# Final adds one output tile later on VectorE, and the last transposes between the two filler pairs

## The chip, the cores and the metric

The kernel runs on one core of one Trainium2 chip. Times are device microseconds (us) of that core. TensorE does matmuls, VectorE, ScalarE and GpSimd do elementwise work, SyncE issues most of the transfers.

Two measures are used. The first is the median device time of several runs. The second is the **tail**, read from the timeline of one profiled execution: it begins at the start of the "first late reciprocal" (the first RECIPROCAL over 2 columns, line L693), which runs when the last attention block is done, and it is read to the end of the last VectorE add and on to the end of the span. The page prints the span to 0.1 us, but the view of a window that runs to the end of the span gives that end to 0.01 us, and the tables and the text use that.

## The reference, cut to what matters

```python
xn = _layernorm(x, axis=-1)                       # x: 1 x 2048 x 512
s  = attention(xn, k_cache, v_cache, wq, wo)      # 32 heads of 128, 2048 keys, then @ wo
g  = silu(relu_glu_mlp(xn, W_gate, W_up, W_down))
return x + s * g
```

The 2048 rows are 16 output tiles of 128 x 512. The heads are worked in 8 groups of 4. For seven groups the projection with `wo` is accumulated in SBUF and folded into `x_sb` early (`x + s_acc * g`). For the last group each output tile is finished by itself: four matmuls into PSUM, a multiply by `g`, an add onto `x_sb`, a store.

## The kernel before

Tiles 0 to 7 of this final stage are mixed into the last attention blocks. Tiles 8 to 15 come after them. Tiles 12 to 15 need the output of the very last attention block, which must be normalised on VectorE, transposed on TensorE and copied to SBUF on ScalarE; tiles 8 to 11 do not need it and serve as filler for TensorE meanwhile.

```python
fin_tmp = [S_([128, D], BF16, "fin_tmp") for _ in range(2)]
# ... (cut)
def emit_final_tile(n, bank):
    # ... (waits, cut)
    for hh in range(G):
        ins = pe.matmul(ps_r[:, bank, 0:D], OT_store[gL % 2][:, hh, n*128:(n+1)*128],
                        Wo_sb[gL % 2][:, hh, :], start=(hh == 0), stop=(hh == G - 1))
    otok = sem_op.sig(ins)
    fb = fin_cnt[0] % NFT                         # NFT = len(fin_tmp)
    fin_cnt[0] += 1
    _wait(dve, otok)
    _wait(dve, fin_free[fb])
    mtok = sem_opa.sig(
        dve.tensor_tensor(fin_tmp[fb][:], ps_r[:, bank, 0:D], g_sb[:, n, :], ALU.mult))   # L787
    _wait(dve, mtok)                              # the add waits for the multiply in front of it
    ftok = sem_opa.sig(
        dve.tensor_tensor(x_sb[:, n, :], x_sb[:, n, :], fin_tmp[fb][:], ALU.add))         # L792
    fin_free[fb] = ftok
    # ... then the store of the tile, or of a pair of tiles, from SyncE
    return mtok                                   # frees the PSUM bank

# ... (cut) after the last attention block:
for n in range(NT - 8, NT - 4, 2):                # tiles 8 to 11, the fillers
    emit_M([(emit_final_tile, n), (emit_final_tile, n + 1)])
flush_last_transposes()                           # TensorE transposes, ScalarE copies
for n in range(NT - 4, NT, 2):                    # tiles 12 to 15
    emit_M([(emit_final_tile, n), (emit_final_tile, n + 1)])
```

`emit_M` takes one of three PSUM slots of two banks each, and waits until its last readers are done.

The softmax here doesn't subtract the row's maximum and nothing guards it: scores larger than these inputs give would overflow.

## Time and profile before

| what | value | view |
|---|---|---|
| median of the first three runs | 1287.48 us (1286.75 to 1287.56) | run times |
| span of the profiled run | 1286.0 us | page |
| share of the chain that ended last on TensorE | 98% | page, part 4 |
| VectorE busy over the whole span | 382.0 us, 30% | page, part 1 |
| VectorE in the tail | from 1274.27 to 1283.91 without a gap | timeline |
| TensorE's last matmul of the tail ends | 1282.08 | timeline |
| end of the span | 1285.96 | window to the end of the span |

The shares over the whole span say "TensorE". They are an average over stages. The final tiles run in the last 30 us (tile 0's multiply starts at 1255.91), what the change can save lies in the last 12, and only the timeline of those tells what limits them. This is VectorE's timeline before the change; columns: start in us, length in us, engine, line and operation, output and inputs, count, and in brackets idle time before it and what ended it. Onorm is the normalised output of the last attention block.

```profile
1274.27 0.17 DVE L693 RECIPROCAL rz_sb<-ps_acc 128x2 f32<-128x2 f32 x1 [0.35 <-PE ps_acc L742]
1274.48 0.42 DVE L696 TENSOR_TENSOR Onorm<-ps_acc,rz_sb 128x256 bf16<-128x256 f32 x1
1274.82 0.16 DVE L693 RECIPROCAL rz_sb<-ps_acc 128x2 f32<-128x2 f32 x1
1275.01 0.42 DVE L696 TENSOR_TENSOR Onorm<-ps_acc,rz_sb 128x256 bf16<-128x256 f32 x1
1275.35 0.68 DVE L787 TENSOR_TENSOR fin_tmp<-ps_r,g_sb 128x512 bf16<-128x512 f32 x1
1276.07 0.42 DVE L792 TENSOR_TENSOR x_sb<-x_sb,fin_tmp 128x512 bf16<-128x512 bf16 x1
1276.41 0.68 DVE L787 TENSOR_TENSOR fin_tmp<-ps_r,g_sb 128x512 bf16<-128x512 f32 x1
...
1282.78 0.68 DVE L787 TENSOR_TENSOR fin_tmp<-ps_r,g_sb 128x512 bf16<-128x512 f32 x1
1283.49 0.42 DVE L792 TENSOR_TENSOR x_sb<-x_sb,fin_tmp 128x512 bf16<-128x512 bf16 x1
```

Read the starts, not only the lengths. From a multiply to its own add it is 1276.07 - 1275.35 = 0.72 us, more than the multiply's 0.68: the add waits for the result. From that add to the next multiply it is 1276.41 - 1276.07 = 0.34 us, less than the add's recorded 0.42: the next operation waits for nothing and starts before the record of this one ends. One tile takes 1.06 us. What 0.72 could be is shown elsewhere in the same trace, where VectorE works through independent operations of the same length back to back, 0.59 to 0.60 us from start to start (the Trainium skill, "Perfetto Trace Analysis", section "DVE / Act Engine Instruction", says that the record runs until the write is acknowledged, while the next operation may begin its fetch earlier). VectorE's timeline before the change, in the first stage:

```profile
21.72 0.67 DVE L460 TENSOR_TENSOR hT<-gr_sb,ps_r 128x512 bf16<-128x512 bf16 x1
22.31 0.69 DVE L319 BATCH_NORM_STATS2 stats<-x_sb 128x6 f32<-128x512 bf16 x1
22.91 0.67 DVE L460 TENSOR_TENSOR hT<-gr_sb,ps_r 128x512 bf16<-128x512 bf16 x1
```

TensorE's timeline before the change, over the same tail:

```profile
1274.19 3.62 PE L779 MATMUL ps_r<-Wo_sb,OT_store 128*128 128x512 bf16 x16
1277.64 0.39 PE L714 MATMUL ps_r<-ident,Onorm 128*128 128x128 bf16 x4
1278.47 3.61 PE L779 MATMUL ps_r<-Wo_sb,OT_store 128*128 128x512 bf16 x16 [0.44 <-ACT OT_store L719]
```

Tiles 8 to 11 (16 matmuls), the four transposes, a wait of 0.44 us for ScalarE's copies, tiles 12 to 15. TensorE is done at 1282.08, while VectorE begins the multiply of the last tile only at 1282.78. TensorE's wait is therefore not what ends the kernel, before the change.

### The profile page before, as it was taken

How to read it: one execution, taken by the hardware profiler on the slowest of the kernel's cores; microseconds unless marked ns; L12 is line 12 of the kernel's file. 1: busy time of each engine (PE TensorE's matmuls, PEld its weight loads, DVE VectorE, ACT ScalarE, POOL GpSimd, SP SyncE). 2: the span in 40 equal slices, each digit the busy share in tenths (PEclk: the TensorE clock that was granted, in tenths of full speed). 3: DMA queues.
4: the chain of work that ended last, by engine and by line, in shares of the span. 5: the costliest groups of instructions: out<-in, count | busy, mean ns of one | idle time of the engine just before them, and what ended most of it. 6: DMA issues, size and time to landing. Idle time of an engine off the chain costs nothing.

```text
span 1286.0 us, 26948 instructions
## 1 busy us (share of the span) xinstructions
PE 1279.3 (99%) x12040; PEld 835.4 (65%) x12040; DVE 382.0 (30%) x685; ACT 1001.7 (78%) x1109; POOL 13.2 (1%) x25
## 2 busy tenths in 40 slices
PE   9999999999999999999999999999999999999998
PEld 5444466666666666666666666666666666666665
DVE  6433311112222222222222222222222222234456
ACT  3322399998888888888888888888888888888884
POOL 2100000000000000000000000000000000000000
PEclk9999999999999999999999999999999999999999
DMA  9600123332222332332221322323323212332302
GB/s 262 131 1 1 21 44 52 63 57 38 37 54 47 71 54 50 55 70 51 54 46 33 64 47 53 55 67 55 55 50 71 54 34 38 52 65 55 50 14 74
DMA packets 240977, 72.13 MB, mean 56 GB/s; under 512 B 227808, under 2 KB 240864, under 8 KB 240864
## 3 DMA queue, kind: packets, MB, share of 16 engines
q1 hardware_dynamic: 240048, 69.76, 28.4%
q8 instruction: 96, 1.57, 0.5%
q10 hardware_dynamic: 816, 0.66, 0.2%
q14 instruction: 17, 0.14, 0.0%
HBM read 32.77 MB, written 2.10 MB: 27 GB/s over the span
## 4 chain that ended last, share of the span: by engine, by line
PE 98%; DVE 1%; DMA 0%; issue 0%; ACT 0%; ACTq 0%
PE ps_acc L742 36%; PE ps_r L645 34%; PE ps_r L578 9%; PE ps_r L599 8%; PE ps_acc L511 4%; PE ps_r L488 4%; PE ps_r L492 4%; PE ps_r L779 1%; DMA Wu_sb<-in_B_W_up_dram 0%; DVE fin_tmp L787 0%; PE ps_r L402 0%; ACT gr_sb L454 0%; DVE x_sb L792 0%; PE ps_acc L364 0%; DVE Onorm L696 0%
## 5 line engine op out<-in xcount | busy, mean ns | idle before, releaser
L655 ACT ACTIVATE PT<-ps_r 128x1024 bf16<-128x1024 f32 x1024 | 952.5, 1054 | 167.7 <-PE ps_r L645 167.7
L742 PEld LDWEIGHTS ps_acc<-V_sb,PT 128*128 128x128 bf16 x8192 | 621.1, 98 | 241.7 <-ACT PT L655 3.5
L742 PE MATMUL ps_acc<-V_sb,PT 128*128 128x129 bf16 x8192 | 776.7, 220 | 0.0
L645 PE MATMUL ps_r<-QT_sb,KT_sb 128*128 128x512 bf16 x2048 | 754.2, 379 | 0.0
L672 DVE RECIPROCAL rz_sb<-ps_acc 128x4 f32<-128x4 f32 x127 | 23.3, 184 | 729.5 <-PE ps_acc L742 729.5
L645 PEld LDWEIGHTS ps_r<-QT_sb,KT_sb 128*128 128x128 bf16 x2048 | 194.9, 98 | 1.1 <-DVE QT_sb L589 0.4
L578 PE MATMUL ps_r<-xnT,Wq_sb 128*128 128x512 bf16 x512 | 130.9, 379 | 0.0
L599 PE MATMUL ps_r<-Wo_sb,OT_store 128*128 128x512 bf16 x448 | 114.6, 379 | 0.0
L589 DVE CAST QT_sb<-ps_r 128x512 bf16<-128x512 f32 x128 | 88.5, 692 | 48.1 <-PE ps_r L578 48.1
L578 PEld LDWEIGHTS ps_r<-xnT,Wq_sb 128*128 128x128 bf16 x512 | 49.9, 97 | 60.6 <-ACT PT L655 27.1
L675 DVE TENSOR_TENSOR Onorm<-ps_acc,rz_sb 128x512 bf16<-128x512 f32 x127 | 87.8, 691 | 4.4
L599 PEld LDWEIGHTS ps_r<-Wo_sb,OT_store 128*128 128x128 bf16 x448 | 43.8, 98 | 52.9 <-ACT PT L655 0.2
L454 ACT ACTIVATE gr_sb<-ps_r 128x512 bf16<-128x512 f32 x56 | 32.9, 595 | 49.9 <-PE ps_r L488 49.3
L612 DVE TENSOR_TENSOR s_acc<-s_acc,ps_r 128x512 f32<-128x512 f32 x96 | 66.0, 688 | 17.3 <-PE ps_r L599 17.3
L460 DVE TENSOR_TENSOR hT<-gr_sb,ps_r 128x512 bf16<-128x512 bf16 x56 | 38.4, 686 | 47.2 <-PE ps_r L492 42.1
L511 PE MATMUL ps_acc<-Wd_sb,hT 128*128 128x512 bf16 x224 | 49.0, 379 | 0.0
L492 PE MATMUL ps_r<-xnT,Wu_sb 128*128 128x512 bf16 x168 | 43.1, 379 | 0.0
L488 PE MATMUL ps_r<-xnT,Wg_sb 128*128 128x512 bf16 x168 | 43.1, 379 | 0.0
L511 PEld LDWEIGHTS ps_acc<-Wd_sb,hT 128*128 128x128 bf16 x224 | 21.9, 98 | 26.4
L519 ACT ACTIVATE sig_sb<-ps_acc 128x512 f32<-128x512 f32 x12 | 7.2, 597 | 29.5 <-PE ps_acc L511 29.5
L488 PEld LDWEIGHTS ps_r<-xnT,Wg_sb 128*128 128x128 bf16 x168 | 16.4, 98 | 19.8
L492 PEld LDWEIGHTS ps_r<-xnT,Wu_sb 128*128 128x128 bf16 x168 | 16.4, 98 | 19.8
(50 smaller groups left out, 182.2 us busy)
## 6 DMA issues: line engine op xcount, KB each, us to landing
V_sb<-in_A_v_cache_dram SPq DMA_DIRECT2D x32, 512.0 KB, 4.8
Wq_sb<-in_A_wq_dram SPq DMA_DIRECT2D x32, 128.0 KB, 2.5
Wo_sb<-in_A_wo_dram SPq DMA_DIRECT2D x8, 512.0 KB, 5.0
OT_store<-Onorm SPq DMA_TRANSPOSE x127, 2.4
Wd_sb<-in_B_W_down_dram SPq DMA_DIRECT2D x1, 1792.0 KB, 14.3
x_sb<-in_A_x_dram SPq DMA_DIRECT2D x3, 512.0 KB, 11.4
out_dram<-x_sb SPq DMA_DIRECT2D x6, 256.0 KB, 2.2
Wg_sb<-in_B_W_gate_dram SPq DMA_DIRECT2D x1, 768.0 KB, 10.9
```

The lines of the kernel that those rows point to most:

```text
L460: dve.tensor_tensor(hT[par][:, fc, :], gr_sb[gk][:], ps_r[:, gb + 1, :], ALU.mult)
L488: ins = pe.matmul(ps_r[:, gb, :], Wg_sb[:, c, fs], xT[:, c, xs], start=(c == 0), stop=(c == DC - 1))
L492: ins = pe.matmul(ps_r[:, gb + 1, :], Wu_sb[:, c, fs], xT[:, c, xs], start=(c == 0), stop=(c == DC - 1))
L511: ins = pe.matmul(ps_acc[:, jb, 0:D], hT[par][:, fc, j * 128:(j + 1) * 128], Wd_sb[:, fc, :], start=(fc == 0), stop=(fc == FC - 1))
L578: ins = pe.matmul(ps_r[:, bank, :], Wq_sb[b][:, c, :], xnT[:, c, qs], start=(c == 0), stop=(c == DC - 1))
L589: etok = sem_qpe.sig(dve.tensor_copy(QT_sb[b][:, qs], ps_r[:, bank, :]))
L599: ins = pe.matmul(ps_r[:, bank, 0:D], OT_store[g % 2][:, hh, n * 128:(n + 1) * 128], Wo_sb[g % 2][:, hh, :], start=(hh == 0), stop=(hh == ...
L612: dve.tensor_tensor(s_acc[:, n, :], s_acc[:, n, :], ps_r[:, bank, 0:D], ALU.add)
L645: ins = pe.matmul(ps_r[:, 2 * s + tt, :], KT_sb[h % 2][:, t * 128:(t + 1) * 128], QT_sb[h % 2][:, qs], start=True, stop=True)
L655: act.activation(PT[pb][:], ps_r[:, 2 * s:2 * s + 2, :], ACTF.Exp, scale=scale)
L675: dve.tensor_tensor(Onorm[ob][:], o_ap, rz_sb[:].to_broadcast([128, 4, Dh]), ALU.mult))
L742: ins = pe.matmul(o_ap, PT[pb][:, tt, j * 128:(j + 1) * 128], V_sb[vb][:, t, 0:VW], start=(t == 0 and j % 2 == 0), stop=(t == KT - 1 and j ...
```

## The change

Its intent: no add shall wait for the operation right in front of it, and TensorE shall not wait for the copies. The number of operations stays the same.

```diff
-fin_tmp = [S_([128, D], BF16, "fin_tmp") for _ in range(2)]
+fin_tmp = [S_([128, D], BF16, "fin_tmp") for _ in range(4)]
@@ in emit_final_tile, after the multiply of tile n
+                    flush_final_add()                 # the add of the tile before
+                    fin_pending.append((n, fb, mtok))
+                    return mtok
+
+                fin_pending = []
+
+                def flush_final_add():
+                    if not fin_pending:
+                        return
+                    n, fb, mtok = fin_pending.pop()
+                    Q, j = divmod(n, 4)
                     _wait(dve, mtok)
                     # ... add and store as before, cut
-                    return mtok
@@ the end of the kernel
                 for n in range(NT - 8, NT - 4, 2):
                     emit_M([(emit_final_tile, n), (emit_final_tile, n + 1)])
-                flush_last_transposes()
+                    if n == NT - 8:
+                        flush_last_transposes()
                 for n in range(NT - 4, NT, 2):
                     emit_M([(emit_final_tile, n), (emit_final_tile, n + 1)])
+                flush_final_add()
```

## The prediction

> **What bounds the kernel now.** The chain of waits puts 98% of the 1286.0 us span on TensorE; the change touches only the last 30 us. There VectorE bounds the end. By the timeline it runs without a gap from 1274.27 to 1283.91 us: reciprocal, Onorm, reciprocal, Onorm, then eight pairs (tiles 8 to 15) of multiply L787 (0.68 us) and add L792 (0.42 us), one tile every 1.06 us. TensorE's last output matmul ends at about 1282.08; the last store lands about 2.1 us after the last add.
>
> **Where the time is in a pair.** Start to start, multiply to its own add takes 0.72 us. Add to the next, independent multiply takes 0.345 us although the add is recorded at 0.42: independent neighbours overlap by about 0.08. Elsewhere in this trace (batch-norm statistics and hT products, 20 to 30 us) an independent successor of a 0.69 us operation starts 0.60 us after it, a dependent one 0.72. The Trainium skill, "VectorE: DVE Perf Modes", section "The DRAIN you can't avoid", says that a semaphore between chained operations costs nothing extra; this trace disagrees by 0.11 us per dependent pair.
>
> **What the change does.** No operation is added or removed. (1) Each add comes one multiply later, so no add but the last waits for the operation right before it. The cadence should fall from 1.06 to 0.60 + 0.345 = 0.95 us per tile; TensorE needs 4 x 0.216 = 0.86, so VectorE stays the limit, barely. (2) The add of tile 7, which now runs before an idle gap of 0.35 us, is pushed behind the multiply of tile 8, into the saturated stretch: plus 0.35. (3) The last transposes (0.23 us on TensorE) go eight matmuls earlier, so the ScalarE copies (0.65 us) hide behind tiles 10 and 11; TensorE loses its wait of 0.44 to 0.6 us near 1278 and ends at about 1281.5. That wait is off the critical path today, but after (1) a late TensorE would become the limit: (3) is what lets (1) pay.
>
> **Sum**, an estimate from these numbers: multiply of tile 8 at 1275.35 as before; then one every 0.95 us, the last at 1282.0; add 14 at 1282.6; add 15 at 1282.95, ending at about 1283.37 instead of 1283.91: 0.54 us less. (Eight tiles x 0.11 = 0.88, less 0.35 for the displaced add.) Adds 14 and 15 are then 0.35 us apart instead of 1.06; one store issue takes SyncE 0.33 us and 128 KB take about 0.5 us at the 253 GB/s seen in the window, so the last store may wait for the one before: give back 0.1 to 0.2 us. Net 0.4 us, to 1287.1 us: 0.03%, less than the spread of the three runs before (0.8 us). Tiles 0 to 7 run in VectorE's slack and give nothing.
>
> Range 1286.3 to 1287.8. Faster by over 2%: 1%; within 2%: 98%; slower by over 2%: 1%.
>
> **What would show it.** Right: multiplies 0.95 us apart in the tail's timeline, adds starting 0.60 after the unrelated multiply, TensorE continuous from 1274.2 to about 1281.5 with the copies under tiles 10 and 11, the last add ending 9.1 us after the first late reciprocal starts, where it was 9.64. Wrong: multiply to add still 0.72 (the change then loses 0.35 us); VectorE idle behind output matmuls; transposes held up by the second Onorm (it ends at 1275.43, TensorE gets there near 1275.9).
>
> **What would make it wrong.** An overlap that holds for other pairs but not for multiply to add; a last store that queues for longer; drift of the whole program by more than the gain.

## The result

| | before | after |
|---|---|---|
| median | 1287.5 us (1286.75 to 1287.57, 6 runs) | 1286.69 us (1286.24 to 1287.28, 6 runs) |
| span of the profiled run | 1285.96 | 1284.64 |
| start of the first score matmul | 144.85 | 144.06 |
| from there to the first late reciprocal | 1129.42 | 1129.42 |
| tail to the last add | 9.64 | 8.96 |
| tail to the end of the span | 11.68 | 11.16 |

The ratio of the times is 0.9995, with a 95% interval from 0.9982 to 1.0008. It is the mean of one kernel's fast runs over that of the other's of the same rounds, so not quite the ratio of the medians. By this alone the kernels are the same. The tail is clearer: it is 0.68 us shorter to the last add and 0.52 us shorter to the end. The two profiled spans differ by more, 1.32 us; the table shows that 0.79 us of that was there before the first score matmul, in code that the change does not touch. Most of it, 0.66 us, comes from one wait; 0.12 us is there one group of matmuls earlier (6.33 against 6.21). TensorE's timeline before the change, at the start of the kernel:

```profile
7.23 0.40 PE L402 MATMUL ps_r<-xcT,Wu_sb 128*128 128x128 bf16 x4 [0.51 <-DMA Wu_sb<-in_B_W_up_dram]
```

and after the change:

```profile
6.45 0.39 PE L402 MATMUL ps_r<-xcT,Wu_sb 128*128 128x128 bf16 x4
```

The first up-weights had landed earlier in that run (5.1 us after their issue, 6.0 before the change). From there on the two executions keep a constant distance of 0.79 us until the tail begins (144.85 against 144.06, 1274.27 against 1273.48).

VectorE's timeline after the change:

```profile
1273.48 0.17 DVE L693 RECIPROCAL rz_sb<-ps_acc 128x2 f32<-128x2 f32 x1 [0.61 <-PE ps_acc L742]
...
1274.56 0.68 DVE L787 TENSOR_TENSOR fin_tmp<-ps_r,g_sb 128x512 bf16<-128x512 f32 x1
1275.15 0.42 DVE L803 TENSOR_TENSOR x_sb<-x_sb,fin_tmp 128x512 bf16<-128x512 bf16 x1
1275.49 0.69 DVE L787 TENSOR_TENSOR fin_tmp<-ps_r,g_sb 128x512 bf16<-128x512 f32 x1
...
1281.09 0.69 DVE L787 TENSOR_TENSOR fin_tmp<-ps_r,g_sb 128x512 bf16<-128x512 f32 x1
1281.69 0.75 DVE L803 TENSOR_TENSOR x_sb<-x_sb,fin_tmp 128x512 bf16<-128x512 bf16 x2
```

The add at 1275.15 is that of tile 7; it starts 0.60 us after the multiply of tile 8, although that multiply is recorded for 0.68. Multiplies are (1281.09 - 1274.56) / 7 = 0.933 us apart. The last line merges the adds of tiles 14 and 15. TensorE's timeline after the change:

```profile
1273.39 1.89 PE L779 MATMUL ps_r<-Wo_sb,OT_store 128*128 128x512 bf16 x8
1275.12 0.39 PE L714 MATMUL ps_r<-ident,Onorm 128*128 128x128 bf16 x4
1275.34 5.34 PE L779 MATMUL ps_r<-Wo_sb,OT_store 128*128 128x512 bf16 x24
```

The wait is gone; TensorE is done at 1280.68, 7.20 us after the first late reciprocal, where it was 7.81 before. The copies ran at 1275.43 for 0.65 us, under the matmuls of tile 10.

### The profile page after: what moved, and what is told of

Its sections match the earlier page's. It is cut to its first block, busy times and chain, and to the rows that moved or that the text cites. A ratio compares the mean times of both kernels' runs of the same rounds, so it can differ in the third digit from the quotient of the medians.

```text
span 1284.6 us, 26946 instructions
## 1 busy us (share of the span) xinstructions
PE 1278.8 (100%) x12040; PEld 835.2 (65%) x12040; DVE 380.6 (30%) x685; ACT 1001.7 (78%) x1109; POOL 13.2 (1%) x25
## 4 chain that ended last, share of the span: by engine, by line
PE 99%; DVE 1%; ACT 0%; issue 0%; DVEq 0%
PE ps_acc L742 36%; PE ps_r L645 34%; PE ps_r L578 9%; PE ps_r L599 8%; PE ps_acc L511 4%; PE ps_r L488 4%; PE ps_r L492 4%; PE ps_r L779 1%; DVE fin_tmp L787 0%; PE ps_r L402 0%; PE ps_r L374 0%; DVE x_sb L803 0%; ACT gr_sb L454 0%; PE ps_acc L364 0%; ACT xcT L369 0%
```

## The experiments

All twelve gave correct results. The last column is the mean of the kernel's runs minus the mean of the runs of the kernel before in the same rounds.

| run | tail to last add | to end of span | first score matmul | median us | mean difference us |
|---|---|---|---|---|---|
| before | 9.64 | 11.68 | 144.85 | 1287.5 | |
| after | 8.96 | 11.16 | 144.06 | 1286.69 | -0.65 |
| e0_after_again | 8.96 | 11.15 | 144.28 | 1286.67 | -0.66 |
| e1_adds_only | 9.41 | 11.61 | 144.01 | 1287.09 | -0.32 |
| e2_transposes_only | 9.64 | 11.68 | 145.06 | 1287.03 | -0.22 |
| e3_wait_back | 9.98 | 12.18 | 144.58 | 1287.87 | +0.40 |
| e4_two_buffers | 10.32 | 12.52 | 145.25 | 1288.46 | +1.05 |
| e5_early_flush | 8.95 | 11.15 | 143.91 | 1286.68 | -0.73 |
| e6_pool_adds | 8.69 | 10.93 | 145.62 | 1286.75 | -0.54 |
| e7_no_filler | 10.30 | 12.50 | 144.22 | 1288.22 | +0.93 |
| e8_pool_early | 8.60 | 10.80 | 144.72 | 1286.52 | -0.77 |
| e9_store_act | 8.96 | 11.08 | 144.05 | 1286.59 | -0.74 |
| e10_both | 8.60 | 10.72 | 144.53 | 1286.48 | -0.79 |
| e11_swap_waits | 9.84 | 12.04 | 144.39 | 1287.79 | +0.56 |

The theory: VectorE bounds the tail; the change takes about 0.12 us of waiting out of each multiply-add pair; moving the transposes keeps TensorE from becoming the limit instead. The rivals: the transposes carry the gain; the later adds alone carry it; the order and not the wait matters; the gain is only when the weights land.

### e0_after_again: what repeats

No edit.

> The changed kernel once more, to see what repeats. Measure used in all runs here: the tail, from the start of the first late reciprocal (the one over 2 columns) to the end of the last VectorE add, and on to the end of the span. Before: 9.64 and 11.73 us; changed kernel: 8.96 and 11.12. Theory (the gain of 0.6 us is the tail, the other 0.8 us between the two profiles is when the first up-weights landed): the tail repeats within 0.05 us, while the start of the first score matmul moves by up to 1 us from run to run. Rival (the body got shorter too): the first score matmul to the first late reciprocal differs between the kernels by more than 0.1 us.

The tail to the last add came out at 8.96 again. From the first score matmul to the first late reciprocal it was 1129.42 us here too, and 1129.42 or 1129.43 in every run of the table, while the first score matmul itself moved between 143.91 and 145.62. So the body did not get shorter, and most of the scatter of the profiled spans is in the head. The part from the last add to the end of the span was 2.19 us here and 2.20 in the first run, so that piece repeats as well.

### e1_adds_only and e2_transposes_only: one part of the change at a time

```diff
 e1_adds_only, against the changed kernel:
-                    if n == NT - 8:
-                        flush_last_transposes()
+                flush_last_transposes()              # behind tile 11 again

 e2_transposes_only, against the changed kernel:
-                    flush_final_add()
                     fin_pending.append((n, fb, mtok))
+                    flush_final_add()                # each add right behind its own multiply
```

> Adds one tile later, but the transposes back behind tile 11. Theory (both parts are needed): TensorE waits again for the ScalarE copies before tile 12, so the multiply of tile 12 starts about 5.26 us after the first late reciprocal instead of 4.81; VectorE is idle there for about 0.45 us; tail 9.4 to the last add, 11.55 to the end of the span. Rival (the later adds alone carry it, TensorE has slack): tail 8.96 and 11.12 as with the whole change.

> Transposes between the filler pairs, but each add right behind its own multiply. Theory (VectorE bounds the tail, TensorE's earlier end is worth nothing alone): tiles 1.06 us apart, tail 9.64 and 11.73 as before the change. Rival (the moved transposes carry the gain): about 9.1 and 11.2.

With the adds alone the tail is 9.41: a gain of 0.23 of the 0.68. The timeline of e1_adds_only shows where the rest went: TensorE waits for ScalarE's copy, and now VectorE waits for TensorE behind it.

```profile
1277.12 0.65 ACT L719 COPY OT_store<-ps_r 128x256 bf16<-128x256 bf16 x2 [5.76 <-PE ps_r L714]
...
1277.63 3.18 PE L779 MATMUL ps_r<-Wo_sb,OT_store 128*128 128x512 bf16 x14 [0.44 <-ACT OT_store L719]
1277.92 0.41 DVE L803 TENSOR_TENSOR x_sb<-x_sb,fin_tmp 128x512 bf16<-128x512 bf16 x1
1278.70 0.69 DVE L787 TENSOR_TENSOR fin_tmp<-ps_r,g_sb 128x512 bf16<-128x512 f32 x1 [0.37 <-PE ps_r L779]
```

With the transposes alone the tail is 9.64, exactly that of before, although TensorE has lost its wait. This run also keeps the four buffers, so they alone give nothing either. The timeline of e2_transposes_only, where the first late reciprocal starts at 1274.48:

```profile
1276.35 5.34 PE L779 MATMUL ps_r<-Wo_sb,OT_store 128*128 128x512 bf16 x24
...
1283.70 0.42 DVE L803 TENSOR_TENSOR x_sb<-x_sb,fin_tmp 128x512 bf16<-128x512 bf16 x1
```

So neither rival holds: the parts give 0.23 and 0.00 alone and 0.68 together. (The mean time of e2_transposes_only was still 0.22 us below before. Its tail is the same, so that is the scatter of the totals, and a difference of that size in the last column should not be read.)

### e3_wait_back: the wait alone

```diff
-                    flush_final_add()
+                    flush_final_add(mtok)            # mtok: the multiply just issued
-                def flush_final_add():
+                def flush_final_add(wtok=None):
-                    _wait(dve, mtok)
+                    _wait(dve, wtok or mtok)
```

> The changed kernel with its order, buffers and transposes, but each late add waits, without need, for the multiply right in front of it. Theory (what a pair pays is the wait on the preceding operation, 0.12 us each): multiply to next add 0.72 again, tiles 1.06 apart, tail about 10.0 and 12.2, worse than before because the add of tile 7 has moved into it. Rival, the Trainium skill's VectorE page taken at its word, that a semaphore between chained operations costs nothing (the order or the reading of a fresh result is what cost): tail 8.96 and 11.12.

Order, buffers and data are those of the changed kernel; the add still reads a result that is one operation older. Only the semaphore value that it waits for is that of the operation in front. VectorE's timeline of e3_wait_back:

```profile
1275.08 0.68 DVE L787 TENSOR_TENSOR fin_tmp<-ps_r,g_sb 128x512 bf16<-128x512 f32 x1
1275.80 0.43 DVE L803 TENSOR_TENSOR x_sb<-x_sb,fin_tmp 128x512 bf16<-128x512 bf16 x1
1276.14 0.68 DVE L787 TENSOR_TENSOR fin_tmp<-ps_r,g_sb 128x512 bf16<-128x512 f32 x1
```

It is 0.72 us again from multiply to add, and the tail of 9.98 is worse than before, because the add of tile 7 has moved into it. The wait itself is the cost: 0.72 - 0.60 = 0.12 us each.

### e4_two_buffers and e11_swap_waits: the buffers, and an order of waits

```diff
 e4_two_buffers, against the changed kernel:
-fin_tmp = [S_([128, D], BF16, "fin_tmp") for _ in range(4)]
+fin_tmp = [S_([128, D], BF16, "fin_tmp") for _ in range(2)]

 e11_swap_waits, against e4_two_buffers:
-                    _wait(dve, otok)
                     _wait(dve, fin_free[fb])
+                    _wait(dve, otok)
```

> The changed kernel with two fin_tmp buffers, as before the change, instead of four. Theory: with two, each multiply needs the buffer that the add right in front of it has just read, so the wait moves from multiply-add to add-multiply: add to multiply 0.46 instead of 0.335, tiles 1.055 us apart, tail about 9.8 to the last add and 12.0 to the end of the span, no better than before. Rival (the buffers are a precaution): 8.96 and 11.12.

The direction was right and the size was not: the tail was 10.32, not 9.8. With two buffers the multiply must wait for the add right in front of it, and that step took 0.52 us, where 0.46 had been expected. VectorE's timeline of e4_two_buffers:

```profile
1276.35 0.41 DVE L803 TENSOR_TENSOR x_sb<-x_sb,fin_tmp 128x512 bf16<-128x512 bf16 x1
1276.87 0.69 DVE L787 TENSOR_TENSOR fin_tmp<-ps_r,g_sb 128x512 bf16<-128x512 f32 x1
```

This multiply has two waits, one for the matmul and one for the buffer. The next run changed only the order in which they are written.

> The two-buffer run again, with the multiply's two waits written in the other order: first for the buffer's free, then for the matmul. In the two-buffer run the add-to-multiply step was 0.52 us, where 0.46 was expected; the built program's listing shows that the wait written last (there: for the add right in front) comes first at the instruction, now the other way round. Theory (a wait on a just finished operation costs more in front of another wait than as the instruction's own): add to multiply 0.45 to 0.46, tiles 1.055 us apart, tail about 9.83 and 12.0. Rival (a fresh wait costs 0.11 there whatever the order, for instance because the multiply reads PSUM): 0.52 again, tail 10.32 and 12.5.

VectorE's timeline of e11_swap_waits:

```profile
1275.49 0.42 DVE L803 TENSOR_TENSOR x_sb<-x_sb,fin_tmp 128x512 bf16<-128x512 bf16 x1
1275.94 0.69 DVE L787 TENSOR_TENSOR fin_tmp<-ps_r,g_sb 128x512 bf16<-128x512 f32 x1
```

The step is 0.45 us, and the tail 9.84. So where two waits are needed and the one on the neighbour is satisfied last, their order is worth 0.52 - 0.45 = 0.07 us each time here. Why is not shown. In either order two buffers are no better than the kernel before: the buffers are a needed part of the change, because with two of them the wait only moves from the add to the multiply. By the code three should do (the multiply of tile n would wait for the add of tile n - 3, two operations before its neighbour); no run tried three.

### e5_early_flush: the displaced add

```diff
+                            flush_final_add()        # the add of tile 7, before the late reciprocals
                             emit_norm_last(b, 0, tx)
                             emit_norm_last(b, 1, ty)
```

> The changed kernel, but the add of tile 7 is issued before the late reciprocals, in VectorE's gap, instead of behind the multiply of tile 8. The prediction counted this displaced add as 0.35 us in the saturated stretch: then the tail is 8.6 and 10.8. Rival, from the changed kernel's trace: the multiply of tile 10 starts 0.05 us after its last matmul ends, so TensorE is as late as VectorE there, and the displaced add costs only about 0.03: tail 8.93 and 11.1, with VectorE now idle in front of the multiplies of tiles 9 and 10.

The rival is right: the tail is 8.95 against 8.96. With the add of tile 7 out of the way, VectorE is ready earlier and waits for TensorE. VectorE's timeline of e5_early_flush:

```profile
1274.41 1.45 DVE L788 TENSOR_TENSOR fin_tmp<-ps_r,g_sb 128x512 bf16<-128x512 f32 x2
1275.78 0.41 DVE L804 TENSOR_TENSOR x_sb<-x_sb,fin_tmp 128x512 bf16<-128x512 bf16 x1
1276.26 0.69 DVE L788 TENSOR_TENSOR fin_tmp<-ps_r,g_sb 128x512 bf16<-128x512 f32 x1
```

From the add at 1275.78 to the multiply of tile 10 at 1276.26 it is 0.48 us, where unhindered it is 0.33. That multiply starts 2.93 us after the first late reciprocal; in the changed kernel it was 2.94. In the changed kernel the four matmuls of tile 10 end at 1275.34 + 3 x 0.216 + 0.38 = 1276.37 (an estimate from the matmul times of the trace) and the multiply starts at 1276.42. The displaced add fills time in which VectorE would have waited anyway.

### e7_no_filler: the transposes before all fillers

```diff
+                flush_last_transposes()
                 for n in range(NT - 8, NT - 4, 2):
                     emit_M([(emit_final_tile, n), (emit_final_tile, n + 1)])
-                    if n == NT - 8:
-                        flush_last_transposes()
```

> The changed kernel with the transposes before tile 8, with no filler at all. Theory (the fillers hide VectorE's reciprocals and norms): TensorE waits about 1.2 us for the second Onorm, the multiply of tile 8 starts about 2.35 us after the first late reciprocal instead of 1.08, tail about 10.2 and 12.4. Rival (TensorE has slack enough to take it): 8.96 and 11.12.

The tail is 10.30 and 12.50, and the multiply of tile 8 starts at 2.41 instead of 1.08. VectorE's wait for TensorE there is 1.24 us, as its timeline of e7_no_filler shows:

```profile
1276.05 0.69 DVE L787 TENSOR_TENSOR fin_tmp<-ps_r,g_sb 128x512 bf16<-128x512 f32 x1 [1.24 <-PE ps_r L779]
```

So of the three places tried, in front of tile 8, behind tile 9 and behind tile 11, the middle one is right: the first makes TensorE wait for VectorE's norms, the last for ScalarE's copies.

### e6_pool_adds and e8_pool_early: taking adds off VectorE

VectorE needs 0.933 us a tile and TensorE 4 x 0.216 = 0.864. What remains between them can be had by giving some adds to GpSimd.

```diff
                     flush_final_add()
+                    if n >= NT - 8 and n % 2 == 0:   # e6; in e8: n in (NT - 8, NT - 6, NT - 3)
+                        if n == NT - 8:
+                            _wait(pool, base_done[NT - 1])
+                        _wait(pool, mtok)
+                        ftok = sem_padd.sig(pool.tensor_tensor(
+                            x_sb[:, n, :], x_sb[:, n, :], fin_tmp[fb][:], ALU.add))
+                        # ... bookkeeping and store, cut
+                        return mtok
                     fin_pending.append((n, fb, mtok))
```

> The changed kernel with the adds of tiles 8, 10, 12 and 14 on GpSimd [...]. Theory (VectorE's 0.935 us a tile against TensorE's 0.865 is what is left): VectorE needs 0.77 a tile, TensorE becomes the limit, multiplies start right behind their matmuls, the last one 7.24 us after the first late reciprocal; tail 8.4 to the last VectorE add and 10.55 to the end of the span. Rival (GpSimd's add is slow, or slows VectorE's SBUF operations): an add over 1.3 us or VectorE adds over 0.45 us, tail over 9.

The tail is 8.69, better than the change by 0.27 but not the 0.56 hoped for. (A passage cut from this expectation gave 0.77 us for a GpSimd add. The operation of that length is a TENSOR_SCALAR in line L345, which reads one tile and not two; no GpSimd add of two tiles was in the trace before this run.) The last multiply started 7.32 us after the first late reciprocal, close to the 7.24 expected, but then the last add took 0.66 us. The timeline of e6_pool_adds:

```profile
1276.72 0.42 DVE L813 TENSOR_TENSOR x_sb<-x_sb,fin_tmp 128x512 bf16<-128x512 bf16 x1
1276.96 1.19 POOL L794 TENSOR_TENSOR x_sb<-x_sb,fin_tmp 128x512 bf16<-128x512 bf16 x1 [1236.85 <-DVE fin_tmp L787]
...
1282.03 0.41 DVE L813 TENSOR_TENSOR x_sb<-x_sb,fin_tmp 128x512 bf16<-128x512 bf16 x1
1282.19 1.26 POOL L794 TENSOR_TENSOR x_sb<-x_sb,fin_tmp 128x512 bf16<-128x512 bf16 x1 [0.46 <-DVE fin_tmp L787]
1282.36 0.69 DVE L787 TENSOR_TENSOR fin_tmp<-ps_r,g_sb 128x512 bf16<-128x512 f32 x1
1283.08 0.66 DVE L813 TENSOR_TENSOR x_sb<-x_sb,fin_tmp 128x512 bf16<-128x512 bf16 x1
```

GpSimd's last add runs from 1282.19 to 1283.45. The VectorE add at 1282.03 had started before it and took the usual 0.41. The multiply at 1282.36, which reads PSUM, ran inside it and took the usual 0.69. The add at 1283.08 started inside it and ended at 1283.74, 0.28 us after GpSimd was done. The Trainium skill, "SBUF — State Buffer", section "SBUF: two separate sides", describes a port pair that the two engines share: the one that starts first holds it for the whole instruction and the other blocks, for VectorE when it has two SBUF inputs and GpSimd's operation reads SBUF, as here. This fits, and e8_pool_early tested it.

> GpSimd takes the adds of tiles 8, 10 and 13 instead of 8, 10, 12 and 14. In the run with GpSimd adds the last VectorE add took 0.66 us instead of 0.42, and it had started while a GpSimd add was still running. Theory (the two engines exclude each other on such adds, as the Trainium skill's SBUF page says of the shared port pair): with GpSimd done about 0.2 us before VectorE's last two adds, both take 0.42; tail 8.6 and 10.8, although VectorE now has one more add to do between the last multiply and the last add. Rival (the last add waits on something else): it takes 0.66 again, tail 8.85 and 11.1.

The timeline of e8_pool_early:

```profile
1280.50 1.26 POOL L794 TENSOR_TENSOR x_sb<-x_sb,fin_tmp 128x512 bf16<-128x512 bf16 x1 [1.40 <-DVE fin_tmp L787]
...
1281.99 0.75 DVE L813 TENSOR_TENSOR x_sb<-x_sb,fin_tmp 128x512 bf16<-128x512 bf16 x2
```

With GpSimd done before VectorE's last two adds, these took 0.75 us together as in the changed kernel (0.42 each, overlapping), all 13 adds on VectorE were between 0.412 and 0.417 us, and the tail was 8.60, although VectorE had one more add to do. This supports the blocking of VectorE, from one instance: the only slow add in these runs is the one that started inside a GpSimd add.

The traces hold more on the other direction, which no expectation looked at. All ten GpSimd adds of e6_pool_adds, e8_pool_early and e10_both start inside a VectorE add, 0.16 to 0.24 us after its start. Each ends 1.01 us after that VectorE add ends, whether its own record is 1.19 or 1.26 us long. So it looks as if GpSimd, too, waits for VectorE's add to finish, as that rule has it, and part of the 1.26 us is that wait. Another page, "GPSIMD Engine Reference", section "Engine selection", gives about a factor of 2 for two-input elementwise work on GpSimd. Here the records are 1.26 against 0.42 us, a factor of 3; without the overlap it is an estimated 1.01 us, a factor of 2.4. No GpSimd add ran clear of VectorE's adds, so its time without waiting is not shown.

### e9_store_act and e10_both: the last two stores

```diff
-                        _wait(sp, ftok)
-                        sem_out.sig(sp.dma_start(out_t[:, n0:n + 1, :], x_sb[:, n0:n + 1, :]))
+                        q = act if n == NT - 2 else sp
+                        _wait(q, ftok)
+                        sem_out.sig(q.dma_start(out_t[:, n0:n + 1, :], x_sb[:, n0:n + 1, :]))
```

> The changed kernel with the store of tile 14 issued from ScalarE's queue. From the end of the last add to the end of the span took 2.09 us before the change and 2.16 to 2.25 in all runs whose last two adds are 0.34 us apart; the last store's issue took 0.44 us there against 0.33. Theory (the second issue collides with the first on SyncE): 2.09 again, tail 8.96 and 11.05. Rival (the two transfers share the DMA engines): still 2.2, tail 8.96 and 11.15.

> Both: GpSimd adds of tiles 8, 10, 13, and tile 14's store from ScalarE's queue. Candidate for the fastest. Theory: tail 8.6 and 10.7, about 1.0 us less than before the change and 0.4 less than the change. Rival (the queue change gives nothing): 8.6 and 10.8.

SyncE's timeline of the changed kernel, its last store:

```profile
1282.51 0.44 SPq L808 DMA_DIRECT2D out_dram<-x_sb  x1
```

and of e9_store_act:

```profile
1282.46 0.33 SPq L809 DMA_DIRECT2D out_dram<-x_sb  x1
```

The last issue is back to 0.33 us, and it begins 0.03 us after the last add instead of 0.07, so on SyncE the collision is gone. What that does to the end of the kernel shows in the ends of the spans, read to 0.01 us. From the last add to the end it was 2.04 us before the change and in e2_transposes_only, 2.19 or 2.20 in all nine runs whose last two VectorE adds are 0.33 or 0.34 us apart and are both stored from SyncE (e8_pool_early among them), and 2.12 in both e9_store_act and e10_both (e6_pool_adds, with a GpSimd add at the end, had 2.23). So the store on ScalarE's queue takes back 0.08 of the 0.16 us. This lies between the theory and the rival. The other 0.08 us remains although SyncE's last issue is as short as before the change and begins as soon after the last add; why is not shown.

e10_both has the shortest tail to the end, 8.60 and 10.72, which is 0.96 us less than before and 0.44 less than the change. Its mean time is 0.79 us below before (ratio 0.9994, 95% interval from 0.998 to 1.0008). It may be called the best by its tail, not by its total.

## Why the prediction was right

- **Time.** 1287.1 us predicted, range 1286.3 to 1287.8; 1286.69 measured. Faster than said by 0.4 us, inside the range, and as predicted no more than the spread of the runs. That says little: the range also holds the median before, 1287.5, and of the 0.81 us between the medians only 0.52 is the tail; the body has the same length in both, so the rest lies in the head, in code that the change does not touch. The tail is the test: predicted 0.54 us less to the last add and 0.4 net, measured 0.68 and 0.52.
- **The wait is what a pair pays.** Right, and shown alone by e3_wait_back. Predicted 0.11 us per pair and a cadence of 0.95; measured 0.12 and 0.933. Over eight tiles (1.060 - 0.933) x 8 = 1.02 us instead of the predicted 0.88. This is the difference between the predicted 0.54 us to the last add and the measured 0.68. The wait itself makes 0.12 of the 0.127 us a tile; the other 0.01 is the step from an add to the next multiply, 0.34 before and 0.33 after, which was not predicted.
- **TensorE's part.** Right: it was predicted to end 7.2 us after the first late reciprocal (1281.5 on the old clock) and ended at 7.20. That its wait was off the critical path before, and would become the limit without the move, is shown by e2_transposes_only (no gain) and e1_adds_only (a third of the gain).
- **The displaced add, plus 0.35 us.** Right as arithmetic on VectorE (1.02 - 0.34 = 0.68), wrong as a cost that could be had back. e5_early_flush took it out and gained 0.01 us, since at tile 10 TensorE is only 0.05 us ahead of VectorE. The prediction compared the two engines by their pace per tile; it should have compared their arrival at each tile.
- **The last store, give back 0.1 to 0.2 us.** From the last add to the end it was 2.04 us before and 2.20 and 2.19 after, so 0.15 to 0.16. The size is right. Of the cause, half is shown: with the store before the last one off SyncE, where the last issue took 0.44 against 0.33 us, 0.08 us came back (e9_store_act, e10_both). The other half stays open.
- **Tiles 0 to 7 give nothing.** Right: 1129.42 us from the first score matmul to the first late reciprocal in both kernels.
- **Drift of the whole program.** Named as a risk, and it was there: 0.79 us between the two profiled runs, from when the first up-weights landed.

## What to carry to other kernels

Where two dependent elementwise operations alternate at the end of a kernel, put an independent one between them, and give the temporaries enough buffers that the wait does not return as a wait for a free buffer. Before counting the gain, compare when each engine arrives at each tile: shortening one engine by 0.12 us a tile is worth only as much as the next engine is ahead. And when the effect is far below the scatter of the total time, look for a stretch of the trace that repeats to 0.01 us, and judge there.

## What the Trainium skill lacked or had wrong

- "VectorE: DVE Perf Modes", section "The DRAIN you can't avoid", says that waits between chained operations cost nothing extra, measured on copies. Here a wait on the preceding operation cost 0.12 us per pair of a multiply from PSUM and an add in SBUF (0.72 against 0.60 us start to start, e3_wait_back against the changed kernel). No run here repeats the copies. The same section does say that an operation which is not held starts earlier, so the page's rule "Minimize op *count*, not sems" (section "Rules for kernel authors") is what misleads here.
- No page that was read tells that the order of two waits of one VectorE instruction matters: 0.52 against 0.45 us for the same step in e4_two_buffers and e11_swap_waits.
